# Transposing query and key images in 32x32 blocks on VectorE in a recurrent-memory attention kernel

## The chip, the cores and the metric

The kernel runs on one core of a Trainium2 chip. A core has TensorE (matrix products into PSUM, eight banks of 128 partitions x 512 float32), VectorE and ScalarE (elementwise work on PSUM and SBUF), GpSimd (POOL, which here issues transfers) and SyncE (SP, which issues transfers too), all with queues of their own that are ordered by semaphores. The metric is the time of one execution on the device in microseconds; the median of three runs is shown.

## The reference

Two kinds of layer alternate, A B A B, each with a layernorm in front and a residual behind. A is attention by segments with a recurrent memory; B is linear attention. The change touches A only. Cut to what matters (2048 tokens of 512 features, 32 heads of 128, segments of 32 tokens, 8 memory tokens):

```python
n_seg = S // seg_len                       # 64
mask = (idx[:, None] < M) | (idx[:, None] >= idx[None, :])
mem = mem0
for s in range(n_seg):
    xs = x[:, s * seg_len:(s + 1) * seg_len, :]
    h = jnp.concatenate([mem, xs], axis=1)             # 8 + 32 tokens
    q = jnp.einsum('btd,dhe->bhte', h, Wq)
    k = jnp.einsum('btd,dhe->bhte', h, Wk)
    v = jnp.einsum('btd,dhe->bhte', h, Wv)
    scores = jnp.einsum('bhqe,bhke->bhqk', q, k) * scale
    scores = jnp.where(mask[None, None], scores, -1000000000.0)
    p = _softmax(scores, axis=-1)
    o = jnp.einsum('bhqk,bhke->bhqe', p, v)
    o = jnp.einsum('bhte,hed->btd', o, Wo)
    mem = o[:, :M, :]
    outs.append(o[:, M:, :])
```

The memory of a segment comes out of the segment before, so the 64 segments of each A layer follow one another.

## The kernel before

Weights stay in SBUF for the whole run. A segment has 40 rows, one column tile of TensorE has 32. So each segment is split: 8 memory tokens and 24 of its own tokens make the block that goes through the recurrence (`hT[:, r2, g]`), and the 8 remaining tokens of four segments are collected in one "left" block (`hT[:, r2, 4]`), which does not depend on the memory and can be computed ahead.

`project` (L787) multiplies one block of 32 tokens with half of a weight matrix: 16 heads. TensorE is used as four column tiles of 32 columns, each with the same 32 tokens as stationary operand. Column tile j takes the four heads 8j+4b to 8j+4b+3 with all 128 features, in four accumulating passes (c) of four matmuls with 512 columns. The result, an image, has a token in each partition of a tile and 4 heads x 128 features along the row.

Scores contract over features, so queries and keys must have features in partitions. `turned` (L800) does this. It evacuates the image to SBUF as bf16 (`evac`, on ScalarE or VectorE, whichever the planner picks), and then either sends it through a DMA transpose on SP's queue (L807), or transposes it on TensorE by the identity, 16 column-tiled matmuls (L816) into another PSUM tile, which a second `evac` copies to `qT` or `kT`. `by_dma` and the last argument of the calls at L1200 and L1203 choose: of a step's four images, the first K image goes by DMA in steps 1 to 62, the second K image and both Q images through TensorE. `relaid` (L824) does the same for left keys and left values, with another order of the copies behind (L834 after a DMA transpose into `xln`, L849 after TensorE). Left values are turned a second time, by DMA (L875) or TensorE (L882). The left blocks go by DMA but for the first block of the second layer and the first two of the first.

The image slots `img` are four for the recurrence (NI) and two for left blocks (NIL).

Scores are taken in `mem_attention` (L917): `left` (L943, own queries of the memory rows against left keys) and `main` (L937, 16 matmuls of 40 columns), then Exp on ScalarE (L954), masks on VectorE (L964), sums on TensorE (L970), logarithm and exponential on ScalarE (L973, L975), values (L980, L983), the product on VectorE (L987), the output projection (L1085) and `next_mem` (L1110), which writes the next memory tokens into `hT`. That is the recurrence. `x_attention`, `left_block` (scores at L894), `residual` with `rows_out` (sum at L1121, transfers by POOL to `dx_sb`), and the B layer's `b_in` and `b_out` run beside it.

The order on each engine is fixed before the launch. `schedule` (L222) is a list planner: it plays the program through with a cost for each operation (`c_act`, `c_dve`, `c_pe4`) and among the ready operations of an engine takes the one with the earliest due time, step x 13.5 plus an offset from the table `OFFSET` (L25), which is looked up by step name and by the operation's number in it. An operation with two possible engines goes to the one that would end it first. Semaphore waits follow from the order.

Of the kernel before, what the change touches and what calls it, by code (L numbers as in the profile page):

```python
# [18 lines left out]
TURN = 1.8  # L19
# [487 lines left out]
def _build_kernel(nc, A_x, A_mem0, A_Wq, A_Wk, A_Wv, A_Wo, A_seg_len, B_wqkv, B_wo, out):  # L507
# [65 lines left out]
    NI = 4  # L573
# [6 lines left out]
    qT = av(1280).rearrange("p (h j x) -> p h j x", h=8, j=4)  # L580
    kT = av(1024).rearrange("p (h j x) -> p h j x", h=8, j=4)
    qTl = av(2 * 1024).rearrange("p (r h j x) -> p r h j x", r=2, h=8, j=4)
    kTl = av(2 * 1024).rearrange("p (r b j g c) -> p r b j g c", r=2, b=2, j=4, g=4)
# [26 lines left out]
    scr_flat = kTl[:, 1].rearrange("p b j g c -> p (b j g c)")  # L610
# [159 lines left out]

    img_no = [0, 0]
# [5 lines left out]
    def a_layer(base, first):  # L777
# [9 lines left out]
        def project(W, key, blk, bkeys, b, urgent):  # L787
            tl = P.tile()
            for c in range(4):

                def mm(pe, c=c):
                    for j in range(4):
                        o = (8 * j + 4 * b) * DH
                        r = pe.matmul(tl.f32()[32 * j:32 * j + 32, 0:512], blk[:, c, :], W[:, c, o:o + 512],  # L794
                                      start=(c == 0), stop=(c == 3), tile_position=(0, 32 * j))
# [4 lines left out]
        def turned(W, key, blk, bkeys, b, dst, dkey, urgent, dma):  # L800

            tl = project(W, key, blk, bkeys, b, urgent)
            k = img_no[urgent] % NI if urgent else NI + img_no[urgent] % NIL
            img_no[urgent] += 1
            nd = evac(img[:, k, :], lambda: tl.f32()[:, :], 512, tiles=[tl], writes=[("img", k)], urgent=urgent)
            if dma:
                add("sp", lambda e: e.dma_start_transpose(dst.rearrange("p h j x -> p h (j x)"), img[:, k, :]), 1.25,  # L807
                    reads=[("img", k)], writes=[dkey], dsem="turn%d" % k, lat=TURN + (0.2 if urgent else 0.6))
                return nd
            tt = P.tile()  # L810

            def tr(pe):
                for i in range(4):
                    for j in range(4):
                        o = 128 * i + 32 * j
                        r = pe.transpose(tt.bf16()[32 * j:32 * j + 32, 128 * i:128 * i + 128], img[:, k, o:o + 32],  # L816
                                         id_sb[:, :], tile_position=(0, 32 * j))
                return r
            add("pe", tr, c_pe(4, 128), reads=[("img", k), "id"], tiles=[tt], urgent=urgent, mode="col")
            evac(dst.rearrange("p h j x -> p (h j) x"), lambda: tt.bf16()[:, 0:512].rearrange("p (n x) -> p n x", x=32), 512,  # L820
                 tiles=[tt], writes=[dkey], rate=2, urgent=urgent)
            return nd

        def relaid(tl, k, out, src, dkey, dma):  # L824

            nd = evac(img[:, k, :], lambda: tl.f32()[:, :], 512, tiles=[tl], writes=[("img", k)])
            n = 512 // len(out)
            if dma:
                add("sp", lambda e: e.dma_start_transpose(xln.rearrange("p (i x) -> p i x", i=4), img[:, k, :]), 1.25,
                    reads=[("img", k)], writes=["xln"], dsem="turn%d" % k, lat=TURN + 0.6)  # L830
                for i, o in enumerate(out):
                    if i:
                        P.again()
                    add(ANY, copy(o, src(xln, i)), {"act": c_act(n, 0, 1), "dve": c_dve(n, 2)}, reads=["xln"], writes=[dkey])  # L834
                return nd
            tt = P.tile()

            def tr(pe):
                for i in range(4):
                    for j in range(4):  # L840
                        o = 128 * i + 32 * j
                        r = pe.transpose(tt.bf16()[32 * j:32 * j + 32, 128 * i:128 * i + 128], img[:, k, o:o + 32],
                                         id_sb[:, :], tile_position=(0, 32 * j))
                return r
            add("pe", tr, c_pe(4, 128), reads=[("img", k), "id"], tiles=[tt], mode="col")
            for i, o in enumerate(out):
                if i:
                    P.again()
                add(ANY, copy(o, lambda i=i: src(tt.bf16()[:, 0:512], i)), {"act": c_act(n), "dve": c_dve(n)}, tiles=[tt],  # L849
                    writes=[dkey])  # L850
            return nd

        def slot_left():
            k = NI + img_no[0] % NIL
            img_no[0] += 1
            return k

        def left_block(G, step):
# [3 lines left out]
            for b in range(2):  # L862
                at(step, "left%d" % b)
                turned(Wq_sb, "Wq", blk, bk, b, qTl[:, r2, 4 * b:4 * b + 4, :, :], ("qTl", r2, b), False, by_dma(step))
                tl = project(Wk_sb, "Wk", blk, bk, b, False)
                relaid(tl, slot_left(), [kTl[:, r2, b].rearrange("p j g (i x) -> p (j g) i x", i=4)],
                       lambda v, _: v.rearrange("p (i n x) -> p n i x", i=4, n=16), ("kTl", r2, b), by_dma(step))
            for b in range(2):
                at(step, "leftv%d" % b)
                tl = project(Wv_sb, "Wv", blk, bk, b, False)  # L870
                k = slot_left()
                relaid(tl, k, [img[:, k, 128 * g:128 * g + 128].rearrange("p (j i x) -> p j i x", j=4, i=4) for g in range(4)],
                       lambda v, g: v.rearrange("p (i j g x) -> p g j i x", i=4, j=4, g=4)[:, g], ("img", k), by_dma(step))
                if by_dma(step):
                    add("sp", lambda e, b=b, k=k: e.dma_start_transpose(vleft[:, r2, b], img[:, k, :]), 1.25,  # L875
                        reads=[("img", k)], writes=[("vl", r2, b)], dsem="turn%d" % k, lat=TURN + 0.6)
                    continue
                tt = P.tile()

                def tr(pe, k=k, tt=tt):  # L880
                    for g in range(4):
                        r = pe.transpose(tt.bf16()[:, 128 * g:128 * g + 128], img[:, k, 128 * g:128 * g + 128], id_sb[:, :])  # L882
                    return r
                add("pe", tr, c_pe(4, 128), reads=[("img", k), "id"], tiles=[tt])
                evac(vleft[:, r2, b].rearrange("p g d -> p (g d)"), lambda tt=tt: tt.bf16()[:, 0:512], 512, tiles=[tt],
                     writes=[("vl", r2, b)], rate=2)
            at(step, "lefts")
            tl = P.tile()
            for b in range(2):
                def mm(pe, b=b):  # L890
                    for g in range(4):
                        o = 32 * (4 * b + g)
                        for j in range(4):
                            r = pe.matmul(tl.f32()[32 * j:32 * j + 32, o:o + 32].rearrange("p (i x) -> p i x", i=4),  # L894
                                          kTl[:, r2, b, j, g, :], qTl[:, r2, 4 * b:4 * b + 4, j, 8 * g:8 * g + 8],
                                          start=True, stop=True, tile_position=(0, 32 * j))
                    return r
# [19 lines left out]
        def mem_attention(s, b):  # L917
# [8 lines left out]
            evac(qT[:, hs, :, 32:40], qTl[:, g2, hs, :, gl], 128, reads=[("qTl", g2, b)], writes=[("qL", b)], rate=4)  # L926
# [7 lines left out]
            def main(pe):  # L934
                for i, hh in enumerate(hhs):
                    for j in range(4):
                        r = pe.matmul(tl.f32()[32 * j:32 * j + 32, 40 * i:40 * i + 40], kT[:, hh, j, :],  # L937
                                      qT[:, hh, j, :], start=True, stop=True, tile_position=(0, 32 * j))
                return r

            def left(pe):
                for j in range(4):
                    r = pe.matmul(tl.f32()[32 * j:32 * j + 32, 160:192].rearrange("p (i x) -> p i x", i=4),  # L943
                                  kTl[:, g2, b, j, g, :], qT[:, hs, j, 0:8], start=True, stop=True,
# [246 lines left out]
        for s in range(NSEG):  # L1191
# [96 lines left out]
    def half(v, b):  # L1288
        return v[:, 4 * b:4 * b + 4, :, :].rearrange("p h j x -> p (h j x)")
# [20 lines left out]
    LEFT = (half(qTl[:, 0], 0), [("qTl", 0, 0)], kTl[:, 0].rearrange("p b j g c -> p (b j g c)").bitcast(F32), [("kTl", 0, 0), ("kTl", 0, 1)])  # L1310
# [135 lines left out]
```

The softmax here doesn't subtract the row's maximum and nothing guards it: scores larger than these inputs give would overflow.

## Time and profile before

| what | before |
|---|---|
| runs | 1759.6 us median of three (1759.03 to 1760.03) |
| span of the profiled execution | 1766.3 us |
| granted TensorE clock | 0.995 of full speed |
| DMA transposes from SP | 356, 3.0 us from issue to landing |
| VectorE, 32x256 bf16 copies within SBUF | 512, 219 ns each |
| ScalarE, 128x512 float32 to bf16 evacuations | 782, 597 ns each |
| ScalarE, 128x384 evacuations of attention output | 149, 490 ns each |
| VectorE, the same | 103, 553 ns each |

The profile is one execution; its groups give an engine, a line, the operation, the operands with their shapes, the number of instructions, the busy time in us, the mean of one in ns, and the idle time of the engine just before them with what ended it. A line can be that of a helper: every evacuation has L623 (ScalarE) or L624 (VectorE). Matmuls overlap in the array, so the time that a group of matmuls takes is read from the distance of starts in the chain of waits and not from the duration of one.

### The profile page before, as it was taken

What the parts mean: (1) busy time and instruction counts of PE and PEld (TensorE: products, weight loads), DVE (VectorE), ACT (ScalarE), POOL (GpSimd) and SP (SyncE); (2) the same over time, 40 slices, a digit from 0 to 9 for tenths busy, and PEclk for the clock granted to TensorE, in tenths of its full rate; (3) what the DMA queues carried; (4) which work ended last, traced back from release to release, by engine and by line L of the source; (5) the groups of instructions that cost most, each with busy time, mean ns of one, the idle gap of its engine ahead of it and who ended that gap; (6) DMA issues with size and microseconds to landing.
All of it is one profiled execution on the core that took longest, in us unless ns stands there. A gap on an engine that the chain in (4) does not pass through costs nothing.

```text
span 1766.3 us, 101302 instructions
## 1 busy us (share of the span) xinstructions
PE 1687.6 (96%) x46178; PEld 1113.7 (63%) x46178; DVE 1133.6 (64%) x3960; ACT 1130.2 (64%) x3069; POOL 329.3 (19%) x660
## 2 busy tenths in 40 slices
PE   5999999999999999999999999999999999999997
PEld 2666666666666666666666666666666666666664
DVE  2566666666666666666566666766666766666666
ACT  3666666666666666666476656666666666666665
POOL 2012211111121112222101211122211112222120
PEclk9999999999999999999999999999999999999999
DMA  9222222222222222222013223222222222222314
GB/s 378 74 37 45 47 44 46 47 42 42 45 46 44 43 51 39 46 48 45 16 31 40 42 45 53 40 48 48 48 45 48 42 48 47 46 48 45 56 29 136
DMA packets 228541, 97.48 MB, mean 55 GB/s; under 512 B 207096, under 2 KB 222256, under 8 KB 226576
## 3 DMA queue, kind: packets, MB, share of 16 engines
q1 hardware_dynamic: 204784, 58.64, 18.3%
q0 software_dynamic: 21744, 19.78, 5.0%
q10 hardware_dynamic: 1584, 12.58, 1.7%
q8 instruction: 361, 5.91, 1.4%
q14 instruction: 68, 0.56, 0.1%
HBM read 29.63 MB, written 10.49 MB: 23 GB/s over the span
## 4 chain that ended last, share of the span: by engine, by line
PE 79%; DMA 9%; DVE 5%; ACT 5%; issue 1%; POOL 1%; ACTq 0%; DVEq 0%
PE pb L794 40%; PE pb L1085 14%; DMA arena_sb<-arena_sb 5%; PE pb L1051 4%; PE pb L816 4%; PE pb L1247 3%; DMA dx_sb<-y_sb 2%; DVE arena_sb L624 2%; PE pb L937 2%; PE pb L1281 2%; ACT arena_sb L623 1%; PE pb L970 1%; DMA Wk_sb<-in_A_Wk_dram 1%; PE pb L1110 1%; PE pb L765 1%
## 5 line engine op out<-in xcount | busy, mean ns | idle before, releaser
L623 ACT ACTIVATE arena_sb<-pb 128x512 bf16<-128x512 f32 (+6 forms) x1375 | 674.6, 509 | 301.1 <-PE pb L794 221.1
L639 POOL DMA_DIRECT2D dx_sb<-y_sb x504 | 256.8, 516 | 1105.1 <-DVE arena_sb L624 489.1
L794 PE MATMUL pb<-Wk_sb,arena_sb 128*32 128x512 bf16 x5120 | 345.3, 381 | 16.4 <-DVE arena_sb L624 7.3
L794 PE MATMUL pb<-Wv_sb,arena_sb 128*32 128x512 bf16 x5120 | 355.5, 379 | 1.8 <-issue 1.7
L1085 PE MATMUL pb<-Wo_sb,arena_sb 128*32 128x256 bf16 x10368 | 331.3, 274 | 10.2 <-DVE arena_sb L987 8.8
L794 PE MATMUL pb<-Wq_sb,arena_sb 128*32 128x512 bf16 x5120 | 340.2, 381 | 0.6 <-DMA Wq_sb<-in_A_Wq_dram 0.6
L1085 PEld LDWEIGHTS pb<-Wo_sb,arena_sb 128*32 128x32 bf16 x10368 | 266.6, 97 | 43.7 <-DVE arena_sb L987 20.3
L624 DVE CAST arena_sb<-pb 128x512 bf16<-128x512 f32 (+3 forms) x459 | 232.7, 519 | 84.9 <-PE pb L794 66.1
L624 DVE COPY arena_sb<-pb 128x512 bf16<-128x512 bf16 (+2 forms) x422 | 150.4, 364 | 171.9 <-PE pb L816 156.4
L624 DVE COPY arena_sb<-arena_sb 32x256 bf16<-32x256 bf16 (+2 forms) x960 | 202.4, 211 | 74.1 <-PE pb L943 18.8
L794 PEld LDWEIGHTS pb<-Wk_sb,arena_sb 128*32 128x32 bf16 x5120 | 131.4, 97 | 121.6 <-DVE arena_sb L624 10.3
L794 PEld LDWEIGHTS pb<-Wq_sb,arena_sb 128*32 128x32 bf16 x5120 | 132.0, 97 | 116.3 <-issue 1.9
L623 ACT ACTIVATE outW_sb<-pb 128x128 fp32r<-128x128 f32 x288 | 79.9, 277 | 161.1 <-PE pb L1085 156.7
L794 PEld LDWEIGHTS pb<-Wv_sb,arena_sb 128*32 128x32 bf16 x5120 | 116.1, 95 | 48.8 <-issue 3.6
L816 PEld LDWEIGHTS pb<-id_sb,arena_sb 128*32 128x32 bf16 x6304 | 110.5, 97 | 53.4 <-DVE arena_sb L624 12.1
L954 ACT ACTIVATE arena_sb<-pb 128x192 bf16<-128x192 f32 (+1 forms) x256 | 81.7, 329 | 94.3 <-PE pb L943 47.8
L816 PE MATMUL pb<-id_sb,arena_sb 128*32 128x128 bf16 x6304 | 135.7, 219 | 0.1
L1121 DVE TENSOR_TENSOR y_sb<-pb,outW_sb 64x256 bf16<-64x256 f32 x158 | 65.8, 417 | 88.8 <-ACT outW_sb L623 86.1
L1051 PE MATMUL pb<-arena_sb 128*128 128x128 bf16 x1024 | 114.4, 221 | 5.7 <-DVE arena_sb L624 4.3
L964 DVE TENSOR_TENSOR arena_sb<-arena_sb 128x128 bf16<-128x128 bf16 x504 | 86.3, 220 | 16.8 <-ACT arena_sb L954 15.6
L1051 PEld LDWEIGHTS pb<-arena_sb 128*128 128x128 bf16 x1024 | 69.8, 97 | 41.3 <-issue 19.8
L987 DVE TENSOR_TENSOR arena_sb<-pb,arena_sb 128x128 bf16<-128x128 f32 x252 | 68.0, 286 | 27.7 <-ACT arena_sb L975 15.3
(125 smaller groups left out, 1996.0 us busy)
## 6 DMA issues: line engine op xcount, KB each, us to landing
arena_sb<-arena_sb SPq DMA_TRANSPOSE x356, 3.0
Wq_sb<-in_A_Wq_dram ACTq DMA_DIRECT2D x1, 4096.0 KB, 13.7
Wk_sb<-in_A_Wk_dram ACTq DMA_DIRECT2D x1, 4096.0 KB, 24.4
Wv_sb<-in_A_Wv_dram ACTq DMA_DIRECT2D x1, 4096.0 KB, 34.8
Wo_sb<-in_A_Wo_dram SPq DMA_DIRECT2D x4, 1024.0 KB, 11.8
xs_scratch<-x_sb POOLq DMA_DIRECT2D x32, 128.0 KB, 2.0
pq_scratch<-arena_sb POOLq DMA_DIRECT2D x32, 128.0 KB, 2.4
dx_sb<-y_sb POOLq DMA_DIRECT2D x252, 12.0 KB, 2.1
```

The lines of the kernel that those rows point to most:

```text
L623: return e.activation(o() if callable(o) else o, i() if callable(i) else i, ACTF.Copy)
L624: return e.tensor_copy(o() if callable(o) else o, i() if callable(i) else i)
L639: add(eng, lambda e: e.dma_start(o, i), 0.55 if eng == "pool" else 0.4, reads=reads, writes=writes, dsem="%s%d" % (kind, k), lat=lat + (0. ...
L794: r = pe.matmul(tl.f32()[32 * j:32 * j + 32, 0:512], blk[:, c, :], W[:, c, o:o + 512], start=(c == 0), stop=(c == 3), tile_position=(0, 32 ...
L816: r = pe.transpose(tt.bf16()[32 * j:32 * j + 32, 128 * i:128 * i + 128], img[:, k, o:o + 32], id_sb[:, :], tile_position=(0, 32 * j))
L954: add("act", lambda a: a.activation(PQ[:, r2, b, 0:nq], tl.f32()[:, 0:nq], ACTF.Exp, scale=SCALE), c_act(nq), tiles=[tl], writes=[("PQ", r ...
L964: add("dve", lambda v, a=a, p_=p_, w_=w_: v.tensor_tensor(wide(Pm[:, k, a, :]), p_.unsqueeze(2).to_broadcast([128, 4, 4, 8]), w_, ALU.mult ...
L987: add("dve", lambda v: v.tensor_tensor(oTb[:, s % NO, 16 * b:16 * b + 16, 0:8], pv.f32()[:, 0:128].rearrange("p (n q) -> p n q", q=8), Rm[ ...
L1051: r = pe.matmul(o, vimg[:, r2, e], Pbx[:, hh, :, :], start=i == 0, stop=False, skip_group_check=True)
L1085: r = pe.matmul(tl.f32()[32 * j:32 * j + 32, 0:256], oT[:, 4 * hh + n, :], Wo_sb[:, 8 * n + hh, 256 * d:256 * d + 256], start=(hh == 0 and ...
L1121: add("dve", lambda v: v.tensor_tensor(y_sb[0:64, k, :], tl.f32()[0:64, 0:256], outW[64:128, w, :].bitcast(F32), ALU.add), c_dve(256), rea ...
L1247: add("pe", lambda pe, c=c: pe.matmul(dst.f32()[:, :], xlnT[:, c, :], wqkv_sb[:, c, o:o + D], start=(c == 0), stop=(c == 3)), c_pe(1, 512) ...
```

## The change

Column tile j now takes features 32j to 32j+31 of all 16 heads of the half, in place of all features of four heads. Tokens are still in the 32 partitions of a tile. A 32x32 block transpose within a tile's 32 partitions then puts feature 32j+f into partition 32j+f, which is where the scores want it. VectorE does such a transpose on 4-byte elements; so two heads are interleaved as neighbouring bf16 values by the evacuation, and one instruction over 256 four-byte elements turns an image. Queries and keys lie in SBUF as pairs (`e`, 2), and the score matmuls read every second element. Left values are turned by two such instructions with a buffer `vtmp` between. `relaid`, the TensorE transposes and the DMA transposes of images are gone; NI is 3.

```diff
-    NI = 4
+    NI = 3
...
-    qT = av(1280).rearrange("p (h j x) -> p h j x", h=8, j=4)
-    kT = av(1024).rearrange("p (h j x) -> p h j x", h=8, j=4)
...
+    qT = av(1280).rearrange("p (h j x e) -> p h j x e", h=8, j=2, e=2)
+    kT = av(1024).rearrange("p (h j x e) -> p h j x e", h=8, j=2, e=2)
+    qTl = av(2 * 1024).rearrange("p (r h j x e) -> p r h j x e", r=2, h=8, j=2, e=2)
+    kTl = av(2 * 1024).rearrange("p (r b g j c) -> p r b g j c", r=2, b=2, g=4, j=2)
+    vtmp = av(512)
...
+    def pairs(v):
+        return v.rearrange("p h j x e -> p (h j) (x e)").bitcast(F32)
...
-        def project(W, key, blk, bkeys, b, urgent):
+        def project(W, key, blk, bkeys, b, urgent, across=False):
...
+                        if across:
+
+                            w = W[:, c, :].rearrange("p (j b i f) -> p b i j f", j=4, b=2, i=4)[:, b, :, :, 32 * j:32 * j + 32]
+                            r = pe.matmul(tl.f32()[32 * j:32 * j + 32, 0:512].rearrange("p (i j f) -> p i j f", i=4, j=4),
+                                          blk[:, c, :], w, start=(c == 0), stop=(c == 3), tile_position=(0, 32 * j))
+                            continue
...
-            if dma:
-                add("sp", lambda e: e.dma_start_transpose(dst.rearrange("p h j x -> p h (j x)"), img[:, k, :]), 1.25,
-                    reads=[("img", k)], writes=[dkey], dsem="turn%d" % k, lat=TURN + (0.2 if urgent else 0.6))
-                return nd
-            tt = P.tile()
...
-            add("pe", tr, c_pe(4, 128), reads=[("img", k), "id"], tiles=[tt], urgent=urgent, mode="col")
-            evac(dst.rearrange("p h j x -> p (h j) x"), lambda: tt.bf16()[:, 0:512].rearrange("p (n x) -> p n x", x=32), 512,
-                 tiles=[tt], writes=[dkey], rate=2, urgent=urgent)
...
+        def turned(W, key, blk, bkeys, b, dst, dkey, urgent, src=None):
+
+            tl = project(W, key, blk, bkeys, b, urgent, True)
+            k = slot_img(urgent)
+            nd = evac(img[:, k, :].rearrange("p (n f e) -> p n e f", f=32, e=2),
+                      lambda: tl.f32()[:, :].rearrange("p (n e f) -> p n e f", f=32, e=2), 512, tiles=[tl],
+                      writes=[("img", k)], urgent=urgent)
+            src = src or (lambda v: v)
+            add("dve", lambda v: v.transpose(dst, src(img[:, k, :].bitcast(F32))), c_dve(256),
+                reads=[("img", k)], writes=[dkey], urgent=urgent)
             return nd
...
+                turned(Wq_sb, "Wq", blk, bk, b, pairs(qTl[:, r2, 4 * b:4 * b + 4]), ("qTl", r2, b), False)
+                turned(Wk_sb, "Wk", blk, bk, b, kTl[:, r2, b].rearrange("p g j c -> p (g j c)").bitcast(F32).rearrange("p (g n x) -> p n g x", g=4, n=8),
+                       ("kTl", r2, b), False, lambda v: v.rearrange("p (i j f) -> p j i f", i=4, j=2))
...
+                evac(img[:, k, :], lambda tl=tl: tl.f32()[:, :], 512, tiles=[tl], writes=[("img", k)])
+                add("dve", lambda v, k=k: v.transpose(
+                    vtmp.bitcast(F32).rearrange("p (g n x) -> p n g x", g=4, n=8),
+                    img[:, k, :].bitcast(F32).rearrange("p (i d f) -> p d i f", i=4, d=2)), c_dve(256),
+                    reads=[("img", k)], writes=["vtmp"])
+                add("dve", lambda v, b=b: v.transpose(vleft[:, r2, b].rearrange("p g d -> p (g d)").bitcast(F32), vtmp.bitcast(F32)),
+                    c_dve(256), reads=["vtmp"], writes=[("vl", r2, b)])
...
-                        r = pe.matmul(tl.f32()[32 * j:32 * j + 32, 40 * i:40 * i + 40], kT[:, hh, j, :],
-                                      qT[:, hh, j, :], start=True, stop=True, tile_position=(0, 32 * j))
+                        r = pe.matmul(tl.f32()[32 * j:32 * j + 32, 40 * i:40 * i + 40], kT[:, hh, j // 2, :, j % 2],
+                                      qT[:, hh, j // 2, :, j % 2], start=True, stop=True, tile_position=(0, 32 * j))
...
-                                  kTl[:, g2, b, j, g, :], qT[:, hs, j, 0:8], start=True, stop=True,
+                                  kTl[:, g2, b, g, j // 2, j % 2::2], qT[:, hs, j // 2, 0:8, j % 2], start=True, stop=True,
...
-                turned(Wk_sb, "Wk", blk, bk, b, kT[:, 4 * b:4 * b + 4, :, :], ("kT", b), True, b == 0 and 0 < s < NSEG - 1)
+                turned(Wk_sb, "Wk", blk, bk, b, pairs(kT[:, 4 * b:4 * b + 4]), ("kT", b), True)
...
-                turned(Wq_sb, "Wq", blk, bk, b, qT[:, 4 * b:4 * b + 4, :, 0:32], ("qT", b), True, False)
+                turned(Wq_sb, "Wq", blk, bk, b, pairs(qT[:, 4 * b:4 * b + 4])[:, :, 0:32], ("qT", b), True)
```

The table of offsets, the planner and the values' projections are as before; the transposes are costed by the planner at `c_dve(256)`, that is 0.42 us.

More of the change, by code (lines that the diff above doesn't have):

```diff
@@ L579, in _build_kernel @@
     vleft = av(2 * 1024).rearrange("p (r b g d) -> p r b g d", r=2, b=2, g=4)
-    qT = av(1280).rearrange("p (h j x) -> p h j x", h=8, j=4)
-    kT = av(1024).rearrange("p (h j x) -> p h j x", h=8, j=4)
-    qTl = av(2 * 1024).rearrange("p (r h j x) -> p r h j x", r=2, h=8, j=4)
-    kTl = av(2 * 1024).rearrange("p (r b j g c) -> p r b j g c", r=2, b=2, j=4, g=4)
+    qT = av(1280).rearrange("p (h j x e) -> p h j x e", h=8, j=2, e=2)
[3 more added lines that the diff above has]
+    vtmp = av(512)
     oTb = av(NO * 1024).rearrange("p (r n x) -> p r n x", r=NO, n=32)
@@ L609, in _build_kernel @@
     SCR = [("kTl", 1, 0), ("kTl", 1, 1)]
-    scr_flat = kTl[:, 1].rearrange("p b j g c -> p (b j g c)")
+    scr_flat = kTl[:, 1].rearrange("p b g j c -> p (b g j c)")
     A8_sb = xv[:, 0:128]
@@ L798, in project, with slot_img @@
             return tl
-        def turned(W, key, blk, bkeys, b, dst, dkey, urgent, dma):
-            tl = project(W, key, blk, bkeys, b, urgent)
+        def slot_img(urgent):
             k = img_no[urgent] % NI if urgent else NI + img_no[urgent] % NIL
             img_no[urgent] += 1
-            nd = evac(img[:, k, :], lambda: tl.f32()[:, :], 512, tiles=[tl], writes=[("img", k)], urgent=urgent)
-            if dma:
-                add("sp", lambda e: e.dma_start_transpose(dst.rearrange("p h j x -> p h (j x)"), img[:, k, :]), 1.25,
-                    reads=[("img", k)], writes=[dkey], dsem="turn%d" % k, lat=TURN + (0.2 if urgent else 0.6))
-                return nd
-            tt = P.tile()
[L812 to L818, printed above, removed]
-            add("pe", tr, c_pe(4, 128), reads=[("img", k), "id"], tiles=[tt], urgent=urgent, mode="col")
-            evac(dst.rearrange("p h j x -> p (h j) x"), lambda: tt.bf16()[:, 0:512].rearrange("p (n x) -> p n x", x=32), 512,
-                 tiles=[tt], writes=[dkey], rate=2, urgent=urgent)
-            return nd
@@ L824, in relaid @@
[L824 to L856, printed above, removed]
+            return k
+        def turned(W, key, blk, bkeys, b, dst, dkey, urgent, src=None):
[7 more added lines that the diff above has]
+                reads=[("img", k)], writes=[dkey], urgent=urgent)
+            return nd
@@ L863, in left_block @@
                 at(step, "left%d" % b)
[L864 to L867, printed above, removed]
+                turned(Wq_sb, "Wq", blk, bk, b, pairs(qTl[:, r2, 4 * b:4 * b + 4]), ("qTl", r2, b), False)
+                turned(Wk_sb, "Wk", blk, bk, b, kTl[:, r2, b].rearrange("p g j c -> p (g j c)").bitcast(F32).rearrange("p (g n x) -> p n g x", g=4, n=8),
+                       ("kTl", r2, b), False, lambda v: v.rearrange("p (i j f) -> p j i f", i=4, j=2))
             for b in range(2):
@@ L870, in left_block @@
                 tl = project(Wv_sb, "Wv", blk, bk, b, False)
[L871 to L886, printed above, removed]
+                k = slot_img(False)
+                evac(img[:, k, :], lambda tl=tl: tl.f32()[:, :], 512, tiles=[tl], writes=[("img", k)])
[5 more added lines that the diff above has]
+                    c_dve(256), reads=["vtmp"], writes=[("vl", r2, b)])
             at(step, "lefts")
@@ L894, in mm @@
                             r = pe.matmul(tl.f32()[32 * j:32 * j + 32, o:o + 32].rearrange("p (i x) -> p i x", i=4),
-                                          kTl[:, r2, b, j, g, :], qTl[:, r2, 4 * b:4 * b + 4, j, 8 * g:8 * g + 8],
+                                          kTl[:, r2, b, g, j // 2, j % 2::2],
+                                          qTl[:, r2, 4 * b:4 * b + 4, j // 2, 8 * g:8 * g + 8, j % 2],
                                           start=True, stop=True, tile_position=(0, 32 * j))
@@ L925, in mem_attention @@
             hs = slice(4 * b, 4 * b + 4)
-            evac(qT[:, hs, :, 32:40], qTl[:, g2, hs, :, gl], 128, reads=[("qTl", g2, b)], writes=[("qL", b)], rate=4)
+            evac(qT[:, hs, :, 32:40, :].rearrange("p h j x e -> p (h j) (x e)"),
+                 qTl[:, g2, hs, :, gl, :].rearrange("p h j x e -> p (h j) (x e)"), 128, reads=[("qTl", g2, b)], writes=[("qL", b)], rate=4)
             at(s, "mem%d" % b)
@@ L1288, in half @@
     def half(v, b):
-        return v[:, 4 * b:4 * b + 4, :, :].rearrange("p h j x -> p (h j x)")
+        return v[:, 4 * b:4 * b + 4].rearrange("p h j x e -> p (h j x e)")
     def b_mid(step, n):
@@ L1309, in _build_kernel @@
     OWN = (e_sb, ["e"], rB_sb, XV)
-    LEFT = (half(qTl[:, 0], 0), [("qTl", 0, 0)], kTl[:, 0].rearrange("p b j g c -> p (b j g c)").bitcast(F32), [("kTl", 0, 0), ("kTl", 0, 1)])
+    LEFT = (half(qTl[:, 0], 0), [("qTl", 0, 0)], kTl[:, 0].rearrange("p b g j c -> p (b g j c)").bitcast(F32), [("kTl", 0, 0), ("kTl", 0, 1)])
     XE = Wq_sb[:, :, :].rearrange("p c f -> p (c f)").rearrange("p (w t d) -> p w t d", w=2, t=16)
```

## The prediction

> **What bounds the kernel now.** I read the page from the top: engine shares, the chain that ended last, then the groups of instructions with different shapes kept apart, one step of the recurrence in the chain of waits, and last what TensorE waited for.
>
> ```profile
> PE 1687.6 (96%) x46178; PEld 1113.7 (63%) x46178; DVE 1133.6 (64%) x3960; ACT 1130.2 (64%) x3069; POOL 329.3 (19%) x660
> ...
> PE 79%; DMA 9%; DVE 5%; ACT 5%; issue 1%; POOL 1%; ACTq 0%; DVEq 0%
> ```
>
> TensorE is busy for 1687.6 of 1766.3 us and idle for 78.7. About 19 of those lie in the first 50 us and 14 in the last 117; between them it idles some 3%. VectorE and ScalarE have a third of their time free. Over such a long stretch only less TensorE work, or more idle TensorE, can move the end. The chain of waits through one step of the recurrence shows the same (start, duration, work):
>
> ```profile
> 317.19 0.11 PE pb L1110 x16
> 317.30 0.12 PE pb L1019 x4
> 317.42 0.03 PE pb L1015 x4
> 317.45 4.75 PE pb L794 x88
> 322.20 0.45 PE pb L816 x32
> 322.65 0.43 PE pb L794 x8
> 323.08 0.22 PE pb L816 x16
> 323.30 0.02 PE pb L943 x4
> 323.32 0.10 PE pb L937 x16
> ...
> 328.86 0.86 PE pb L794 x16
> 329.72 0.11 PE pb L1110 x16
> ```
>
> From one L1110 (the next memory tokens) to the next are 12.53 us, TensorE all the way. In it stand three groups of 16 column-tiled transposes (L816), 0.45 us for two and 0.22 for one, so 0.225 us a group. A projection (16 matmuls, L794) takes 0.86.
>
> Is the recurrence itself shorter than that? Its own work, from the rows: cast of the memory tokens 0.19, four K and Q projections 3.44, last evacuation 0.60, transposes and copy 0.22 + 0.42, scores 0.12, Exp 0.33, two masks 0.44, sums 0.11, Ln 0.28, Exp 0.31, product 0.29, output projection 1.75, two evacuations 0.55, L1110 0.28: 9.3 us without the hand-overs between engines. Some 3 us less the hand-overs are filled by other TensorE work. So the step is set by TensorE's throughput, with the recurrence not far below.
>
> The prices of operations:
>
> ```profile
> L1085 PE MATMUL pb<-Wo_sb,arena_sb 128*32 128x256 bf16 x10368 | 331.3, 274 | 10.2 <-DVE arena_sb L987 8.8 <-ACT arena_sb L623 0.8 <-issue 0.3
> ...
> L624 DVE CAST arena_sb<-pb 128x512 bf16<-128x512 f32 x222 | 151.8, 690 | 67.6 <-PE pb L794 66.1 <-PE pb L1055 1.0 <-PE pb L1303 0.3
> L816 PE MATMUL pb<-id_sb,arena_sb 128*32 128x128 bf16 x6304 | 135.7, 219 | 0.1
> ...
> L624 DVE COPY arena_sb<-pb 128x512 bf16<-128x512 bf16 x311 | 127.3, 420 | 163.3 <-PE pb L816 156.4 <-PE pb L943 3.2 <-PE pb L882 1.5
> ...
> L623 ACT ACTIVATE arena_sb<-pb 128x512 bf16<-128x512 bf16 x127 | 75.3, 596 | 25.0 <-PE pb L816 22.4 <-PE pb L842 0.6 <-PE pb L882 0.2
> ...
> L1026 DVE TENSOR_TENSOR arena_sb<-arena_sb 128x256 bf16<-128x256 bf16 x128 | 54.4, 425 | 38.1 <-ACT arena_sb L1024 36.8
> ...
> L1019 PE MATMUL pb<-arena_sb,bo_sb 128*32 128x256 bf16 x512 | 37.8, 275 | 0.1
> ```
>
> The reader is to see the count of L816, the two copies that follow it on either engine, and that L1019, which streams its 256 columns in runs of 32 elements, costs what the contiguous L1085 costs.
>
> **TensorE work removed.** 6304/16 = 394 groups at L816, 192/16 = 12 at L842 (192 matmuls, 220 ns) and 6 groups of four at L882 (24 matmuls, 221 ns). 406 x 0.225 = 91.4 us, and 6 x 0.22 = 1.3: **-92.7 us**, 0.72 a step over 128 steps. All of it lies on the bounding engine.
>
> **Projections with runs of 32.** The moving operand of every K and Q projection now takes 32 features of 16 heads: 64-byte runs. L1019 does the same at 275 against 274 ns, so I take 0. What that row leaves out is the longer jump between runs (2 KB between some heads against 80 bytes). The other end, a halved stream, would add 640 tiles x 0.86 = 550 us; the row excludes anything like it at short jumps, and I keep that end only as a rival.
>
> **Scores with every second element.** L937, L943 and L894 read keys and queries at a step of two. No row has a 2-byte operand at such a step. Sixteen score matmuls and four for the left rows take 0.12 us per half; between 0 and double, that is 0 to 256 x 0.12 = 31 us, and L894 (8 of 32 columns, 1024 matmuls) adds about 3: 0 to 34. I take 0, by L1019 and L1015, which stream broken patterns at full rate.
> Against the change speaks a rule of the Trainium skill, SBUF — State Buffer, Specifications: a 16-byte line wants at least two hits for full bandwidth, and each new line costs. A step of two 2-byte elements leaves four hits a line, so the rule would still add nothing; by half rate the sum would be 34 us higher. No run so far shows it.
>
> **VectorE transposes added.** Per layer 64 steps x 4 and 16 left blocks x 8 (two Q, two K, two V of two each): 384, in all 768, each 256 four-byte elements a lane. None is in the trace. Nearest is L1026, 256 elements a lane at 425 ns; above it the 512-element cast with 690, below it the 32x256 copy with 219. I take 425: 768 x 0.425 = 326 us; ends 168 and 530.
> The Trainium skill, VectorE: DVE Perf Modes, The three transpose paths, gives 311 ns for a 128x128 bf16 transpose. With 128 more elements at that page's 0.96 GHz I estimate 444 ns, 341 us in all. The measured row is used until a run shows a transpose.
>
> **Copies removed.** Of 438 copies of transposed tiles, 406 go: VectorE about 288 x 0.409 = 118 us, ScalarE 118 x 0.593 = 70. The copies behind the DMA transposes go too: 58 of 128x512 (VectorE 8, ScalarE 18) and 232 of 128x128 (32 and 21). VectorE: 1134 - 158 + 326 = 1302 us; ScalarE 1130 - 109 = 1021. Over a span of 1707 that is 76% and 60%, and 222 casts of 690 ns are free to move to ScalarE at 597. At 425 ns neither becomes the bound. Cost 0, hidden under TensorE's 11.8 us a step; without cover see the second rival.
>
> **Evacuations that write every second element** (640). The 128x384 evacuation in runs of 24 takes 490 ns on ScalarE and 553 on VectorE, in line with 597 and 690 for 512, so broken writes cost nothing there. I take 0; doubled writes would add 640 x 0.6 = 384 us to two engines with more free than that.
>
> **DMA transposes removed.** 356 leave SP's queue; no load of the steady state stands behind them. What TensorE itself lost to them:
>
> ```profile
> PE pb L1085 <- DVE arena_sb L987: 8.8, 33, 0.7
> PE pb L937 <- DMA arena_sb<-arena_sb: 8.7, 18, 0.8
> ```
>
> 8.7 us, and 13.4 more as weight loads that waited while matmuls still ran. What is late next is the transpose on VectorE, so I take 0; ends -22 and 0. **Buffers**: three image slots for four. A slot is rewritten three projections later, 2.6 us; free unless VectorE falls that far behind. vtmp has its writer and reader on one engine.
>
> **The new wait and the order.** Each transpose waits for its evacuation, often on ScalarE, and runs on VectorE alone. Behind a waiting one stand VectorE's casts, the masks L964, the products L987 and the sums L1121 for which POOL's transfers wait. The planner lays out all instructions anew with unchanged offsets. Price: from 0 to one cast of 0.69 us ahead of the last transpose of every step with nothing to fill it, 128 x 0.69 = 88 us. V projections (1.72 us) stand ready in that place now, so I take a little over a third: **+33**.
>
> **Sum.** On the profiled span: 1766.3 - 92.7 + 33 = 1706.6. The profiled execution is 6.7 us above the median of the runs (1759.6), so **1700 us**; this case by itself runs from 1675 to 1740.
>
> **Rivals.** *All of the gain* (0.14): no new idle time, perhaps the 22 us of DMA waits too: 1667 to 1645. For it: VectorE has room, and the recurrence shortens from 0.64 to 0.43 us at this point. Against: 128 steps would have to keep their order.
> *VectorE's queue gates the scores* (0.17, the slower side): before each score matmul a cast and a transpose of another block stand ahead, 0.69 + 0.43 = 1.12 us, uncovered: 1667 + 143 = 1810; half covered 1739. It decides from 0.72 us a step, where the saved transposes are spent. For it: up to 10 us of VectorE work in a step of 12; against: fillers.
> *The transpose costs 690 ns* (0.09): VectorE 1134 - 158 + 530 = 1506 us, 85 to 88% busy; Q's two transposes add 0.53 us a step to the recurrence, 68 us: 1768 with the order's 33.
> *A broken pattern is slower than L1019 says* (0.05): scores alone 1734; projections a fifth slower, 110 us more: 1810.
>
> **How the numbers follow.** The forecast has the remaining 0.55. Slower: two thirds of the queue rival, two thirds of the dear transpose, and half of the last: 0.11 + 0.06 + 0.03 = 0.20. A difference under 0.2% (3.5 us) can't be told from none by these runs; that strip of the middle cases gets 0.03, and faster 0.77. The range 1655 to 1770 leaves out the lower half of the full gain and the upper parts of the slow rivals, about 0.2.
>
> **What will show it.** Right: L816, L842 and L882 gone, TensorE busy near 1595 us, L794 still at 379 to 381 ns, a transpose near 425 to 445 ns, VectorE near 1300, TensorE idle near 110. Wrong: TensorE waiting for VectorE's transposes by over 90 us in total, L794 or L937 longer, or a transpose of 0.6 us and more.

## The result and the profile after

The changed kernel takes 1790.2 us in the median of four runs (1786.9 to 1790.7), against 1759.8 for the kernel before: 1.0166 times as long, 95% interval 1.0144 to 1.0188. The forecast was 1700. All the matmuls that were to leave TensorE have left it, and the time went up.

The page of the changed kernel, engine shares and the chain that ended last:

```profile
span 1788.4 us, 87740 instructions
...
PE 1650.6 (92%) x39658; PEld 1006.4 (56%) x39658; DVE 1172.5 (66%) x3916; ACT 1206.4 (67%) x3161; POOL 326.5 (18%) x660
...
PE 74%; ACT 11%; DVE 9%; DMA 2%; issue 2%; POOL 1%; ACTq 0%; DVEq 0%
```

TensorE issues 39658 matmuls in place of 46178. 92.7 us of matmuls are gone, but its busy time fell by 37 only. Matmul spans overlap: 16 projection matmuls of 381 ns each start within 0.86 us. So a stall of some 0.2 us between two starts still counts as busy, and the same instructions make 1595.8 to 1650.6 us of busy time in the orders tried below. The stalls are seen better in the chain, where ScalarE and VectorE now hold 20% in place of 10% (and DMA 2% in place of 9%), and in TensorE's idle time, 137.8 us in place of 78.7.

The groups of the changed kernel with shapes kept apart; L801 is the projection of keys and queries, L805 that of values, L824 the new transpose, L900 the scores:

```profile
L625 ACT ACTIVATE arena_sb<-pb 128x512 bf16<-128x512 f32 x907 | 621.6, 708 | 230.3 <-PE pb L801 150.1 <-PE pb L805 48.0 <-PE pb L1018 4.8
L801 PE MATMUL pb<-Wq_sb,arena_sb 128*32 128x512 bf16 x5120 | 338.4, 381 | 0.8 <-DMA Wq_sb<-in_A_Wq_dram 0.6
...
L824 DVE STREAM_TRANSPOSE arena_sb<-arena_sb 128x256 f32<-128x256 f32 x640 | 284.0, 444 | 317.6 <-ACT arena_sb L625 300.5 <-ACT st_sb L759 13.2
...
L900 PE MATMUL pb<-arena_sb 128*32 128x40 bf16 x4096 | 68.5, 181 | 0.4
```

The projections in runs of 32 cost 381 ns as before, the scores at a step of two 181 against 180. A transpose is 444 ns. The price that moved most is ScalarE's evacuation: 708 ns in the mean over 907 of them (two clusters in the trace: 605 key or query images near 0.76 us, the rest near 0.60), where the 782 of before took 597 in the mean.

What the extra time looks like is seen step by step. The next view gives engine busy time in four consecutive steps of the recurrence in the changed kernel, from one L1073 (next memory tokens; L1110 before) to the next; the first number after the stretch is its length:

```profile
core 0: us, PE busy (x) PEld busy (x) DVE busy (x) ACT busy (x) POOL busy (x), PEclk, DMA share, GB/s
334.67:345.75 11.08, 10.70 (x304) 7.11 (x301) 8.38 (x27) 8.76 (x23) 1.45 (x3) 1.00 0.02 5
345.75:358.45 12.70, 12.07 (x323) 8.04 (x323) 8.04 (x31) 7.69 (x22) 1.64 (x5) 1.00 0.05 16
358.45:369.54 11.09, 9.93 (x250) 5.76 (x248) 7.26 (x29) 7.11 (x21) 5.02 (x10) 1.00 0.07 21
369.54:387.57 18.03, 17.43 (x370) 10.23 (x372) 12.31 (x39) 14.37 (x37) 1.58 (x3) 1.00 0.04 12
```

Three steps are short and one is 18 us long. The kernel before had 14.07, 12.36, 12.22 and 12.53 us in such a group (from one L1110 to the next, from 278.4 us on): less uneven, and 51.2 us against 52.9. This group is the worse sort. A step of some 18 us stands six times in the changed kernel, in every second group of the first layer; the groups between end in a step of 15 us, and in the second layer no step is longer than 15.2 us. Groups of four take longer than before in both layers all the same: 52.6 against 51.6 us in the first and 53.4 against 52.6 in the second, in the mean of 48 steps each. In the third step TensorE is idle for 1.16 of 11.09 us: it has 250 matmuls, little beside the recurrence, and waits for the recurrence's work on other engines. In the fourth it has 370, and the recurrence stands behind them. The chain of waits within that fourth step (start, duration, work):

```profile
376.50 0.13 PE pb L906 x4
376.63 0.11 PE pb L900 x15
376.74 0.65 PE pb L805 x12
377.39 0.86 PE pb L801 x16
...
378.65 0.12 PE pb L933 x2
378.77 1.29 PE pb L1210 x6
380.06 0.98 PE pb L801 x16
381.04 0.87 PE pb L1048 x32
381.91 0.22 PE pb L805 x4
382.13 0.86 PE pb L801 x16
382.99 0.86 PE pb L805 x16
383.86 0.27 PE pb L1014 x3
384.13 0.08 PE pb L1228 x4
384.21 0.07 PE pb L943
384.29 0.09 PE pb L946 x4
```

Between the softmax sums of the second half (L933, 378.65) and its value product (L943, 384.21) TensorE works 5.4 us without a pause. Of all that the product needs one thing: the last pass of the step's own value projection, whose 32 matmuls come as 16, 12 and 4, the 4 at 381.91 (0.22 us), itself held back. The output projection's first half (L1048, 0.87 us) belongs to the recurrence too. The other 4.3 us are filler, that is, work beside the recurrence: the left block (L801 and L805 in sixteens), the B layer's input (L1210, L1228) and attention rows that are not urgent (L1014). The projection's second half and the next memory tokens wait for this product. So filler holds the recurrence up here, while TensorE stood idle in the step before.

### The profile page after: what moved, and what is told of

Its sections match the earlier page's. It is cut to its first block, busy times and chain, and to the rows that moved or that the text cites. A ratio compares the mean times of both kernels' runs of the same rounds, so it can differ in the third digit from the quotient of the medians.

```text
span 1788.4 us, 87740 instructions
## 1 busy us (share of the span) xinstructions
PE 1650.6 (92%) x39658; PEld 1006.4 (56%) x39658; DVE 1172.5 (66%) x3916; ACT 1206.4 (67%) x3161; POOL 326.5 (18%) x660
## 4 chain that ended last, share of the span: by engine, by line
PE 74%; ACT 11%; DVE 9%; DMA 2%; issue 2%; POOL 1%; ACTq 0%; DVEq 0%
PE pb L801 31%; PE pb L805 13%; PE pb L1048 12%; ACT arena_sb L625 4%; PE pb L1210 3%; PE pb L1014 3%; DVE arena_sb L626 3%; PE pb L900 2%; PE pb L1244 2%; DMA Wk_sb<-in_A_Wk_dram 1%; DVE arena_sb L950 1%; PE pb L1073 1%; DMA dx_sb<-y_sb 1%; DVE arena_sb L989 1%; POOL dx_sb L641 1%
## 5 line engine op out<-in xcount | busy, mean ns | idle before, releaser
L625 ACT ACTIVATE arena_sb<-pb 128x512 bf16<-128x512 f32 (+5 forms) x1459 | 781.9, 565 | 282.9 <-PE pb L801 150.1
L824 DVE STREAM_TRANSPOSE arena_sb<-arena_sb 128x256 f32<-128x256 f32 x640 | 284.0, 444 | 317.6 <-ACT arena_sb L625 300.5
L801 PE MATMUL pb<-Wk_sb,arena_sb 128*32 128x512 bf16 x5120 | 337.3, 382 | 33.9 <-ACT arena_sb L625 20.5
L1048 PE MATMUL pb<-Wo_sb,arena_sb 128*32 128x256 bf16 x10368 | 328.1, 275 | 41.9 <-DVE arena_sb L950 39.0
L801 PE MATMUL pb<-Wq_sb,arena_sb 128*32 128x512 bf16 x5120 | 338.4, 381 | 0.8 <-DMA Wq_sb<-in_A_Wq_dram 0.6
L805 PE MATMUL pb<-Wv_sb,arena_sb 128*32 128x512 bf16 x5120 | 335.4, 378 | 0.0
L1048 PEld LDWEIGHTS pb<-Wo_sb,arena_sb 128*32 128x32 bf16 x10368 | 261.9, 97 | 83.1 <-DVE arena_sb L950 56.5
L801 PEld LDWEIGHTS pb<-Wk_sb,arena_sb 128*32 128x32 bf16 x5120 | 128.6, 97 | 156.0 <-ACT arena_sb L625 27.2
L801 PEld LDWEIGHTS pb<-Wq_sb,arena_sb 128*32 128x32 bf16 x5120 | 139.3, 97 | 132.4 <-issue 3.2
L626 DVE CAST arena_sb<-pb 128x384 bf16<-128x384 f32 (+3 forms) x329 | 156.3, 484 | 67.2 <-PE pb L1018 31.4
L626 DVE COPY arena_sb<-arena_sb 32x256 bf16<-32x256 bf16 (+1 forms) x657 | 137.1, 209 | 42.3 <-PE pb L900 24.0
L805 PEld LDWEIGHTS pb<-Wv_sb,arena_sb 128*32 128x32 bf16 x5120 | 117.9, 95 | 81.7 <-ACT arena_sb L987 1.7
L917 ACT ACTIVATE arena_sb<-pb 128x192 bf16<-128x192 f32 (+1 forms) x256 | 81.4, 324 | 68.4 <-PE pb L900 67.8
L1014 PE MATMUL pb<-arena_sb 128*128 128x128 bf16 x1024 | 97.1, 222 | 9.9 <-DVE arena_sb L626 9.1
L927 DVE TENSOR_TENSOR arena_sb<-arena_sb 128x128 bf16<-128x128 bf16 x504 | 86.4, 210 | 9.4 <-ACT arena_sb L917 9.0
L1014 PEld LDWEIGHTS pb<-arena_sb 128*128 128x128 bf16 x1024 | 67.0, 98 | 43.9 <-issue 20.7
L950 DVE TENSOR_TENSOR arena_sb<-pb,arena_sb 128x128 bf16<-128x128 f32 x252 | 70.5, 284 | 28.6 <-ACT arena_sb L938 13.3
L938 ACT ACTIVATE arena_sb<-arena_sb 128x128 f32<-128x128 f32 x252 | 75.9, 319 | 0.8
L641 POOL DMA_DIRECT2D pq_scratch<-arena_sb x32 | 17.8, 557 | 310.1 <-DVE arena_sb L1197 261.7
## 6 DMA issues: line engine op xcount, KB each, us to landing
Wo_sb<-in_A_Wo_dram SPq DMA_DIRECT2D x4, 1024.0 KB, 12.3
```

The costliest lines, as they stand in the source:

```text
L625: return e.activation(o() if callable(o) else o, i() if callable(i) else i, ACTF.Copy)
L626: return e.tensor_copy(o() if callable(o) else o, i() if callable(i) else i)
L641: add(eng, lambda e: e.dma_start(o, i), 0.55 if eng == "pool" else 0.4, reads=reads, writes=writes, dsem="%s%d" % (kind, k), lat=lat + (0. ...
L801: r = pe.matmul(tl.f32()[32 * j:32 * j + 32, 0:512].rearrange("p (i j f) -> p i j f", i=4, j=4), blk[:, c, :], w, start=(c == 0), stop=(c ...
L824: add("dve", lambda v: v.transpose(dst, src(img[:, k, :].bitcast(F32))), c_dve(256), reads=[("img", k)], writes=[dkey], urgent=urgent)
L917: add("act", lambda a: a.activation(PQ[:, r2, b, 0:nq], tl.f32()[:, 0:nq], ACTF.Exp, scale=SCALE), c_act(nq), tiles=[tl], writes=[("PQ", r ...
```

## The experiments

Two theories stood against each other. The **order theory**: the operations are worth what was computed, but the planner's table of offsets was drawn up for the former list of instructions; with another list the same offsets put filler where it harms. The **operation theory**: the new operations cost what was saved, above all the evacuation that writes every second element.

### Both kernels without the table

```diff
-            if nd.key is not None and OFFSET:
+            if False:
```

Priorities are then the longest remaining path. First the kernel before, then the changed one:

> The kernel before, with the planner's table of offsets left out: each operation's priority is the longest remaining path behind it. Same work, another order. Order theory (the change is worth its saved TensorE time, and the loss comes from a table drawn up for the former list of operations): much slower than 1760, by 50 us or more, since the table does that much for the kernel before. Operation theory (the new operations themselves cost what was saved, above all the evacuation that writes every second element, 0.76 us on ScalarE in place of 0.60): no statement on this run alone; it is the base for the next.

> The changed kernel, planned in the same way without the table, so neither kernel has a table made for it. Order theory: faster than the run before it by 60 us or more, 93 if all the saved TensorE time comes through. Operation theory: not faster than it by more than 20 us, slower perhaps.

1904.6 and 1730.5 us, one run each beside 1762.7 for the kernel before. Planned alike, the changed kernel is 174 us faster, and it is faster than the kernel before with its table. Both wait some 24 us for Wq at the start, so their difference is free of that. TensorE's wait for one engine stands out; first without the change, then with it (engine and line, what it waited for, us in total, times, longest):

```profile
PE pb L1085 <- DVE arena_sb L987: 46.8, 84, 1.7
PE pb L794 <- DMA Wq_sb<-in_A_Wq_dram: 24.1, 1, 24.1
```

```profile
PE pb L801 <- DMA Wq_sb<-in_A_Wq_dram: 24.2, 1, 24.2
PE pb L1048 <- DVE arena_sb L950: 15.4, 46, 0.7
```

The output projection's wait for the recurrence's last product (L987, now L950) fell by 31 us. The operation theory had allowed 20 us in all and is out as the main cause. That the difference is 174 and not 93 is more than the order theory asked; how the other 81 divide between the shorter recurrence and the planner's choices is not settled. So this pair shows the sign of the change under one rule for both, and not its size.

### The price of the writes at a step of two

```diff
-            nd = evac(img[:, k, :].rearrange("p (n f e) -> p n e f", f=32, e=2),
-                      lambda: tl.f32()[:, :].rearrange("p (n e f) -> p n e f", f=32, e=2), 512, tiles=[tl],
+            nd = evac(img[:, k, :],
+                      lambda: tl.f32()[:, :], 512, tiles=[tl],
```

> The changed kernel in its own order, but the evacuations of key and query images write contiguously; the interleaving of head pairs is left out, so the scores are taken from other elements. ScalarE's evacuations should fall from 0.76 to 0.60 us, some 617 x 0.16 = 100 us of ScalarE time. Operation theory: 1790 falls by 30 us or more, to 1760 or below. Order theory: it falls by less than 15 us, since the order stays.

1783.2 us (1.0117 of the kernel before, 1.0096 to 1.0138): 7 us less by the medians, 9 by the two ratios. The same group in this kernel:

```profile
L625 ACT ACTIVATE arena_sb<-pb 128x512 bf16<-128x512 f32 x907 | 538.6, 597 | 287.2 <-PE pb L801 190.5 <-PE pb L805 52.5 <-PE pb L906 18.4
```

The group's busy time falls by 83 us (907 x 0.111 = 101 us of durations, which overlap in part), and the time by 7 to 9: about a tenth of it lay on the path that sets the end. The same edit in the order without the table:

> The changed kernel planned without the table (1730), same order, with evacuations that write contiguously; the interleaving of head pairs is left out. It shows the price of the writes at a step of two where no misfit of the table hides it. Order theory: 0 to 20 us less than 1730. Operation theory: 30 us less or more.

1728.6 us (two runs), against 1730.5 (one run): 2 us, which so few runs can't tell from none. It is far from the 30 of the operation theory.

### Interleaving in PSUM

```diff
-                            r = pe.matmul(tl.f32()[32 * j:32 * j + 32, 0:512].rearrange("p (i j f) -> p i j f", i=4, j=4),
-                                          blk[:, c, :], w,
+                            r = pe.matmul(tl.f32()[32 * j:32 * j + 32, 0:512].rearrange("p (i d f e) -> p i d e f", i=4, d=2, e=2),
+                                          blk[:, c, :], w.rearrange("p i (d e) f -> p i d e f", e=2),
```

> The changed kernel in its own order with the interleaving moved: TensorE writes the head pairs interleaved into PSUM (every second float32), the evacuation is contiguous, the output is the reference's. If writing PSUM at a step of two costs TensorE nothing, it lies within 5 us of the run before it and the projection matmuls stay at 379 to 382 ns; if it halves them, 640 x 0.86 = 550 us more. Operation theory: as fast as the run before it, so a gain over 1790 of 30 us or more. Order theory: under 15 us.

2317.2 us (1.3142, 1.3121 to 1.3164), 534 us above the contiguous run before it. The projections of the changed operands in this kernel, beside the values' that still write contiguously:

```profile
L801 PE MATMUL pb<-Wq_sb,arena_sb 128*32 128x512 bf16 x5120 | 623.1, 634 | 0.5 <-DMA Wq_sb<-in_A_Wq_dram 0.3
...
L805 PE MATMUL pb<-Wv_sb,arena_sb 128*32 128x512 bf16 x5120 | 334.3, 380 | 0.0
```

The halved stream that the prediction had kept as the other end for reading, 640 x 0.86 = 550 us, is what was measured for writing. The interleaving belongs to the evacuation.

### One group of filler 25 us later

```diff
-                nd.prio = -(step * PERIOD + OFFSET[name][k])
+                nd.prio = -(step * PERIOD + OFFSET[name][k] + 25.0 * (name == "bi"))
```

`bi` is the B layer's input, all of it filler. On the changed kernel, and as a control on the kernel before:

> The changed kernel with one edit to the due times: the 32 operations of the B layer's input (projections, phi, sums; all filler beside the recurrence) come due 25 us later. No operation is other than in the changed kernel. Order theory: any such edit can move the time by tens of us, since the table no longer fits; this one should bring 1790 to 1750 or below, at or under the kernel before. Operation theory: within 10 us of 1790, since every evacuation, transpose and matmul costs what it did.

> A control: the kernel before, with the edit that helped the changed kernel (the 32 operations of the B layer's input due 25 us later). Same work. Order theory: the table fits this kernel, so the same edit hurts here: 1800 or above. Rival (the edit is good by itself, for any kernel of this make): below 1760.

The changed kernel falls to 1752.9 us (0.9942 of the kernel before, 0.9926 to 0.9959), 37 less with the very same operations, if not quite to the 1750 that was expected; the kernel before rises to 1909.5 (1.085, 1.0809 to 1.0892), 149 more. The edit is not good by itself; one table fits, the other does not.

The planner's own reckoning, made before a launch, agrees. It ends at 1748.7 us for the kernel before and 1794.3 for the changed one. Each single entry of the table moved by 150 us either way gives 1030 alterations that could be played through: for the kernel before not one ends more than 0.2 us earlier, for the changed kernel 8 in 100 end over 1 us earlier, the best by 37. These are the planner's numbers, not the chip's.

### Told the measured costs

```diff
-            nd = evac(img[:, k, :].rearrange("p (n f e) -> p n e f", f=32, e=2),
-                      lambda: tl.f32()[:, :].rearrange("p (n e f) -> p n e f", f=32, e=2), 512, tiles=[tl],
-                      writes=[("img", k)], urgent=urgent)
+            nd = add(ANY, copy(img[:, k, :].rearrange("p (n f e) -> p n e f", f=32, e=2),
+                               lambda: tl.f32()[:, :].rearrange("p (n e f) -> p n e f", f=32, e=2)),
+                     {"act": 0.76, "dve": 0.70}, tiles=[tl], writes=[("img", k)], urgent=urgent)
...
-            add("dve", lambda v: v.transpose(dst, src(img[:, k, :].bitcast(F32))), c_dve(256),
+            add("dve", lambda v: v.transpose(dst, src(img[:, k, :].bitcast(F32))), 0.445,
```

> The changed kernel, where the planner is told what the trace shows: 0.76 us on ScalarE and 0.70 on VectorE for an evacuation that writes every second element, 0.445 for a transpose, in place of 0.60, 0.69 and 0.42. The table stays. More evacuations go to VectorE and the order changes. Theory that wrong costs spoil the plan: 1760 or below. Order theory: somewhere between 1735 and 1800, for the table still does not fit; it can't say where.

1728.8 us (0.9804, 0.9785 to 0.9824), 61 us less. That is what the theory of wrong costs asked (1760 or below), and 6 us under the range of the order theory (1735 to 1800). By itself it does not tell wrong costs from a misfit, since a new cost makes a new order. Two other numbers speak against wrong costs as the main cause: with evacuations at the cost that the planner had been told, and the order unchanged, the kernel took 1783.2 us; and the planner, reckoning with the costs that it believed, put the changed kernel's end at 1794.3 us itself.

### A table made for the changed kernel, and TensorE's time put back

The measured costs and new offsets, found by random alterations kept where the planner's end came earlier; no operation differs from the changed kernel. Then the same order, with nearly as much TensorE time added as the recurrence's transposes took: 384 groups of four matmuls issued twice, 384 x 0.215 = 82.6 us, for 384 x 0.225 = 86.4.

```diff
-                    for j in range(4):
+                    for more, j in [(m, j) for m in range(int(across and urgent and c == 0 and (W is Wq_sb or b == 1)), -1, -1) for j in range(4)]:
...
-                                          blk[:, c, :], w, start=(c == 0), stop=(c == 3), tile_position=(0, 32 * j))
+                                          blk[:, c, :], w, start=(c == 0), stop=(c == 3 or more == 1), tile_position=(0, 32 * j))
```

> The changed kernel with the measured costs and a table made for it by a random search over the planner's own end. No operation is other than in the changed kernel. Order theory: all or most of the saved 93 us come through: 1670 to 1700, TensorE busy near 1596 and idle below 110. Operation theory: not below 1728, where the kernel with the measured costs and the old table lies.

> The run before it, same order, with the saved TensorE time put back: the second K image and both Q images of each step issue their first four matmuls twice (384 x 0.215 = 83 us of TensorE, where the kernel before had its transposes; the first result is overwritten). If TensorE's throughput is what bounds, the time rises by 60 to 85 us. If the recurrence's waits bound it, the projections stand on that chain too and the rise is the same, but TensorE's idle time stays; if other work sets the end, under 30.

1688.6 us (0.9604, 0.959 to 0.9618), 72 us less than the kernel before; and 1766.1 us (1.0032, 1.0021 to 1.0044) with TensorE's time put back, a rise of 77.5 for 82.6 put in. Both pages:

```profile
span 1685.9 us, 87776 instructions
...
PE 1603.7 (95%) x39658; PEld 1015.9 (60%) x39658; DVE 1270.1 (75%) x4055; ACT 1104.3 (66%) x3022; POOL 326.8 (19%) x660
```

```profile
span 1761.3 us, 90848 instructions
...
PE 1684.1 (96%) x41194; PEld 1058.2 (60%) x41194; DVE 1273.2 (72%) x4055; ACT 1112.0 (63%) x3022; POOL 327.1 (19%) x660
```

TensorE's idle time is 82.2 and 77.2 us, as in the kernel before (78.7). In this order nearly each microsecond of TensorE work in that place is one of time. The place is in the recurrence, where the transposes stood too, and the idle time stayed; so the run does not tell TensorE's throughput as the bound from the length of the recurrence. The kernel before had no like search here. Moving single entries gained it nothing by the planner's reckoning; how far a search would take it is not shown, and the 72 us hold against its own table. Four steps of the fitted order, in the view shown above:

```profile
313.96:326.07 12.11, 12.11 (x304) 7.35 (x300) 8.77 (x28) 8.10 (x22) 1.00 (x2) 1.00 0.02 5
326.07:338.95 12.88, 12.64 (x380) 9.33 (x377) 9.51 (x34) 9.37 (x25) 1.66 (x4) 1.00 0.06 16
338.95:349.73 10.78, 10.03 (x253) 6.14 (x253) 9.17 (x32) 6.84 (x22) 5.48 (x11) 1.00 0.08 21
349.73:362.58 12.85, 12.80 (x296) 7.77 (x300) 10.22 (x32) 9.30 (x28) 1.59 (x3) 1.00 0.05 15
```

48.6 us for four steps in place of 52.9. The heavy step has shrunk from 18.03 to 12.85 us and from 370 matmuls to 296, the second step has grown from 323 to 380, and most of TensorE's idle time is in the third.

## Why the prediction was wrong

The step that failed is **the new wait and the order**: +33 us, from 0 to 88. Against the spans the changed kernel shows 1788.4 - (1766.3 - 92.7) = +114.8 us, and by the medians of the runs 1790.2 - (1759.8 - 92.7) = +123. Some 7 to 9 of them are the evacuation's writes; so about 108 (by spans) for this term, over the upper bound. The bound was drawn for another thing. It priced one cast ahead of the last transpose in each step, a wait of the scores for VectorE. TensorE's idle time before the readers of a transpose is small (changed kernel, TensorE's waits for VectorE's L824 and for the product L950):

```profile
PE pb L1048 <- DVE arena_sb L950: 39.0, 86, 1.4
...
PE pb L855 <- DVE arena_sb L824: 1.5, 1, 1.5
PE pb L906 <- DVE arena_sb L824: 1.1, 4, 0.4
```

2.6 us of idle TensorE in the whole run. But idle time is not all of a wait: a weight load (PEld) can be held while the matmuls ahead of it still count as busy. Held weight loads of the kernel before, of the changed one, and of the one with the fitted table:

```profile
PEld pb L943 <- DVE arena_sb L624: 20.9, 70, 2.7
PEld pb L1085 <- DVE arena_sb L987: 20.3, 69, 0.8
...
PEld pb L937 <- DMA arena_sb<-arena_sb: 13.4, 21, 1.1
```

```profile
PEld pb L906 <- DVE arena_sb L824: 60.7, 161, 0.8
PEld pb L1048 <- DVE arena_sb L950: 56.5, 100, 1.6
```

```profile
PEld pb L906 <- DVE arena_sb L824: 45.6, 163, 1.7
...
PEld pb L1048 <- DVE arena_sb L950: 13.8, 28, 2.0
```

So the wait that was priced did come: transposes held the scores' weight loads for 60.7 us, where copies and DMA transposes had held them for 20.9 and 13.4. It is not what made the 108: with the B layer's input 25 us later it was 68.4 us, and the time 37 us less. What goes with the time is how long the recurrence's last product held the output projection: 56.5 us in the changed kernel, 45.8 with that filler later, 13.8 with the fitted table. (A held weight load spans the idle time of TensorE behind the same wait, so the two are not added.)

What happened is that the plan of all engines was made anew from offsets that no longer suited: the same operations took 1752.9 and 1688.6 us in other orders. The bunched filler of the 18 us steps is one form of it, seen in six steps; what lengthens the second layer's steps was not followed up. The text said that the planner lays out all instructions anew with unchanged offsets, and then costed only one consequence of it. With a fitted table the same term is 1685.9 - 1673.6 = +12.3 us (21 by the medians): it can be anything from there to over 110, and no row of the profile before that was shown bounds it.

The other steps, in their order. **TensorE saving**, -92.7: right; the busy time falls to 1603.7 in the fitted order (1595 forecast), and 82.6 us put back cost 77.5. **Projections in runs of 32** and **scores at a step of two**, 0 each: right, 381 and 181 ns, which is also what the line rule of the Trainium skill, SBUF — State Buffer, Specifications, had let expect for a step of two. **Transposes**: 444 ns for 425, 768 of them 340 us for 326; the estimate from figures of the Trainium skill (VectorE: DVE Perf Modes, The three transpose paths) was the better one, 444. In the denser orders the mean of L824 is lower, 431 with the fitted table. **VectorE's load** of 1302 us: 1172 in the changed kernel, since nearly all image evacuations went to ScalarE (1206, forecast 1021); 1270 and 1104 in the fitted order. Neither became the bound. **Evacuations**, 0: wrong in price, 597 to about 760 ns on ScalarE (the row that stood for it, 128x384, writes runs of 24 and not every second element), small in time, 7 to 9 us here and 2 in the other order. **DMA transposes**, 0: their waits are gone, and the weight loads of the scores wait for VectorE in their place, as said. The lower end of -22 was a misreading: in the trace 8.6 of the 8.7 us of idle TensorE lie within the 13.4 us of held weight loads, so the end was -13.4 and that of the full gain 1654.

Of the rivals, the queue of VectorE gating the scores gave 1810, as did slower projections, and so came nearest in number. The projections kept their price. The queue's wait is there, 60.7 us or 0.47 a step for the 1.12 of the rival, but with the later filler it grew while the time fell by 37 us; that the number came near is luck. The full gain was not reached by any order tried. Room on VectorE for a dearer transpose was not tried.

## What to carry to other kernels

Where the order of instructions comes from a planner with hand- or search-made priorities, a change to the list of instructions is two changes, and the second can be larger than the first: here -93 us of work and +108 of order. Fit the priorities anew for both programs before judging the operations; one neutral rule for both gave the right sign here, but 174 us for 93 of removed work. Where a profile shows the bounding engine nearly full, its removed work is worth its time only if the order keeps it full. Like steps of uneven length, and work that is held for the last link of a recurrence, are where to look.

## What the runs showed of the hardware

TensorE writing PSUM at a step of two float32 takes 634 ns for 381 (512 columns, four column tiles), and the whole kernel 534 us more. Reading its moving operand in 64-byte runs with jumps of 2 KB (381 against 381 ns), or both operands at a step of two (181 against 180 ns), costs nothing that shows. ScalarE pays for bf16 writes at a step of two, about 760 for 597 ns. VectorE pays less: with the fitted table its 339 casts of 128x512 lie in two clusters, near 690 ns as before and near 750. A block transpose of 256 four-byte elements a lane has a mean of 444 ns in the changed kernel, 431 with the fitted table and 418 without a table.
